# Attention values take a detour: rows scattered to DRAM by an index column, then read back

## The chip, the cores and the metric

The program runs on one core of one Trainium2 chip. The metric is device time in microseconds for one execution; lower is better. The five engines are written as in the profile: PE is the matrix engine, PEld its weight loads, DVE the vector engine, ACT the scalar engine, POOL the general-purpose engine, and SP the engine that issues most transfers. Each engine works through its own instruction list in order, and so does SP with its transfers: an instruction that waits holds up everything behind it on the same engine.

## The reference, cut to what matters

```python
# q, k, v: (4, 8, 768, 64) float32; proj: (64, 6)
q_bucket = sum((q @ proj > 0) * powers); k_bucket = the same for k
scores = where(q_bucket == k_bucket, q @ k.T / 8, -1e9)
attn = softmax(scores)
attn_out = attn @ v                       # v enters here, and only here
x = attn_out rearranged to (3072, 512)
out = relu(x @ w_in) ** 2 @ w_out         # 512 -> 2048 -> 512
```

There are 4 x 8 = 32 heads. For each head the values `v` are a matrix of 768 rows of 64 floats, that is of 256 bytes a row.

## The kernel before, in words

The kernel has two stages. The first is attention. It takes the 32 heads as 16 pairs (`pr` = 0 to 15), and each pair in 6 steps, one for each tile of 128 keys (`kt` = 0 to 5), so the stage is a loop over 96 steps `u` = 6 `pr` + `kt`. The second stage is the two products with `w_in` and `w_out`, written as a Strassen-like scheme of 128x256 products; nearly all of its time is PE (line 554).

The order of the work is written out by hand in the loop at lines 486 to 522. In step `u` stand, in this order: a running sum of exponentials on DVE (`add_up`, line 343); at `kt` = 0 the loads of queries and keys of pair `pr` + 2 (`load_pair`, eight transfers on SP, line 240); at `kt` = 2 the load of the values of pair `pr` + 1 (`load_values`, line 251); the scores of this step on PE (`score`, line 325) and their exponentials on ACT (line 330); preparation of the next pair's features; and the product with the values of the step two earlier (`attend`, line 353). So `attend(pr, 0)`, the first use of the values of pair `pr`, stands in step 6 `pr` + 2. When a pair is through, `normalize` (line 408) scales its output on DVE and stores it with one transfer on SP to `x_all` in DRAM (line 412).

Between these the stage also loads and rounds the weights of the second stage: 32 pieces, two for each pair. `load_weight` is one transfer on SP (line 122) into a ring of three buffers, so a load waits until DVE has rounded an earlier piece (`round_weight`, lines 159 to 166).

SP therefore sees, for each pair, always the same run of transfers: the values of the next pair, two weight pieces, four query and four key loads, the store of a finished pair's output, and then the values of the pair after. POOL does nothing after the first five microseconds: it makes the identity and other constants and loads `proj` twice (line 192).

`p_v`, the pool of the value tiles, has two buffers for each name.

Of the kernel before, what the change touches and what calls it, by code (L numbers as in the profile page):

```python
# [8 lines left out]
FP32 = mybir.dt.float32  # L9
BF16 = mybir.dt.bfloat16  # L10
I32 = mybir.dt.int32
U32 = mybir.dt.uint32
# [22 lines left out]
def kernel(  # L35
# [10 lines left out]
    nc = tc.nc  # L46
    PSUM = bass.MemoryType.PSUM

    B, H, S, D = q.shape
# [3 lines left out]
    P = 128  # L53
    SB = S // P
# [23 lines left out]
    p_d = ctx.enter_context(tc.tile_pool(name="p_d", bufs=1, space=bass.MemoryType.DRAM))  # L78
# [13 lines left out]
    p_v = first.enter_context(tc.tile_pool(name="p_v", bufs=2))  # L92
    const = first.enter_context(tc.tile_pool(name="const", bufs=1))
# [86 lines left out]
    lifts = const.tile([P, 1], FP32, name="lifts")  # L180
    excess = const.tile([P, 1], FP32, name="excess")
    ones = const.tile([P, 32], FP32, name="ones")
    picks = const.tile([P, P], FP32, name="picks")
    which = const.tile([P, 2, HS // 32], FP32, name="which")
    NRING = 4
# [2 lines left out]
    def constants():  # L188
        N = NBITS
        nc.gpsimd.memset(projs, 0.0)  # L190
        for h in range(2):
            nc.gpsimd.dma_start(out=projs[h * D:(h + 1) * D, 0:N], in_=proj)
        for t in (gains, lifts):
            nc.vector.memset(t, 0.0)
        nc.vector.memset(excess, -896.0)
        for h in range(2):
            r = h * D
            nc.vector.memset(gains[r:r + N + 1], -FAR / 2 * N)
            nc.vector.memset(gains[r:r + N], FAR / 2)
            nc.vector.memset(lifts[r:r + N + 1], 1.0)  # L200
            nc.vector.memset(lifts[r:r + N], -SMALL)
        nc.vector.memset(ones, 1.0)
        for e in ring:
            nc.vector.memset(e[:, :, S:S + 1], TINY)


        for g in range(4):
            cut = picks[:, g * 32:(g + 1) * 32]
            at = 64 * (g // 2)
            nc.gpsimd.tensor_tensor(  # L210
                out=cut, in0=ident[:, at:at + 32], in1=ident[:, at + 32:at + 64], op=ALU.add
            )
        nc.gpsimd.memset(which, 0.0)
        for g in range(4):
            nc.gpsimd.memset(which[g * 32:(g + 1) * 32, g % 2], 1.0)
# [6 lines left out]
    def load_first():  # L222

        for src, name in ((q, "q_nat"), (k, "k_nat")):
            t = p_qk.tile([P, SB, 2, D], FP32, name=name)
            for h in range(2):
                nc.sync.dma_start(
                    out=t[:, :, h], in_=src[0, h].rearrange("(p t) d -> p t d", t=SB)
                )
            nat[0, name] = t  # L230

    def load_pair(pr):


        b, j = divmod(pr, PB)
        for src, name in ((q, "q_nat"), (k, "k_nat")):
            t = p_qk.tile([P, S], FP32, name=name)
            for g in range(4):
                h, e = divmod(g, 2)
                nc.sync.dma_start(  # L240
                    out=t[g * 32:(g + 1) * 32].rearrange("i (t n d) -> i t n d", t=SB, n=P // 32),
                    in_=src[b, 2 * j + h].rearrange(
                        "(n i t) (e d) -> e i t n d", i=32, t=SB, e=2
                    )[e],
                )
            nat[pr, name] = t

    def load_values(pr):
        b, j = divmod(pr, PB)
        t = p_v.tile([P, 2, SB * D], FP32, name="v_nat")  # L250
        nc.sync.dma_start(
            out=t, in_=v[b, 2 * j:2 * j + 2].rearrange("h (p t) d -> p h (t d)", t=SB)
        )
        nat[pr, "v_nat"] = t

    def first_features(w, r):
# [214 lines left out]

    with tc.manual_schedule():
        load_first()
        load_values(0)
        make_identity(nc, ident)
        constants()
        for pr in range(1, AHEAD):
            load_pair(pr)
        for w in range(2):
# [6 lines left out]
        for u in range(len(steps) + 1):  # L486
            if 1 <= u <= len(steps):
                add_up(*steps[u - 1])
            if u < len(steps):
                pr, kt = steps[u]  # L490
                if kt == 0 and pr + AHEAD < NP:
                    load_pair(pr + AHEAD)
                if kt == 2 and pr + 1 < NP:
                    load_values(pr + 1)
                score(pr, kt)
# [398 lines left out]
```

## Time and profile before

| | us |
|---|---|
| median of 2 runs | 1002.38 (1002.13 to 1002.62) |
| the profiled execution, its own time | 1004.74 |
| the profiled execution, span from its first to its last instruction | 1002.6 |
| first stage, from the start to about | 407 |
| PE busy | 954.4 |
| DVE busy | 552.3 |
| ACT busy | 370.5 |
| POOL busy | 3.3 |

The span is what the profile's page divides into engines, slices and groups; the time of the execution is a little more than the span. The granted clock of PE was 0.992 of full speed over the whole run. In the lists of transfers, "us to landing" is the time from issue on the engine to the arrival of the last byte as its semaphore shows it.

### The profile page before, as it was taken

To read this page: it belongs to the slowest core of one execution; us is meant where nothing else is said; L and a number is where in the kernel's file an instruction comes from. 1 tells how busy PE (TensorE), PEld (TensorE's weight loads), DVE (VectorE), ACT (ScalarE), POOL (GpSimd) and SP (SyncE) were. 2 spreads that over 40 slices of the span, in tenths; PEclk is the share of its full clock that TensorE was granted. 3 is DMA by queue.
4 is the path that set the end of the run, shared out by engine and by line. 5 is a ranking of instruction groups with operands and counts; after the bars stand their busy time and mean duration, and the time that the engine had idled before them with its cause. 6 is when DMAs were issued, how large, how long until landed. Compare 5 with 4: busy or idle time off the path is not lost.

```text
span 1002.6 us, 12942 instructions
## 1 busy us (share of the span) xinstructions
PE 954.4 (95%) x5166; PEld 661.2 (66%) x5166; DVE 552.3 (55%) x1070; ACT 370.5 (37%) x689; POOL 3.3 (0%) x18
## 2 busy tenths in 40 slices
PE   6999999998889999899999999999999999999897
PEld 3333333333333333688888888888888888888786
DVE  1677777767777777795048406830682077116500
ACT  4666666665656665331023102300320132013200
POOL 1000000000000000000000000000000000000000
PEclk9999999999999999999999999999999999999999
DMA  8144545553553731001022102210311122000000
GB/s 188 29 115 112 113 107 127 130 125 97 116 139 84 157 122 37 17 1 42 22 76 72 43 22 85 63 53 22 90 49 63 29 71 90 22 22 1 1 22 23
DMA packets 121154, 70.11 MB, mean 70 GB/s; under 512 B 99328, under 2 KB 104448, under 8 KB 121088
## 3 DMA queue, kind: packets, MB, share of 16 engines
q1 hardware_dynamic: 121024, 69.22, 26.3%
q8 instruction: 42, 0.69, 0.3%
q14 instruction: 24, 0.20, 0.1%
q0 software_dynamic: 64, 0.00, 0.0%
HBM read 54.53 MB, written 14.68 MB: 69 GB/s over the span
## 4 chain that ended last, share of the span: by engine, by line
PE 63%; DVE 3%; ACT 1%; DMA 0%; issue 0%; SPq 0%; DVEq 0%; ACTq 0%
PE acc L554 58%; PE xo L353 2%; PE st L325 2%; DVE total L343 1%; PE tot L371 1%; DVE feat L273 0%; DVE x_t L408 0%; DMA q_nat<-in_q_dram 0%; DVE one L163 0%; DVE power L159 0%; PE near L285 0%; ACT small L147 0%; ACT power L148 0%; DVE flip L377 0%; DVE g L645 0%
## 5 line engine op out<-in xcount | busy, mean ns | idle before, releaser
L554 PE MATMUL acc<-x,w_in 128*128 128x256 f32 x768 | 174.7, 379 | 0.0
L330 ACT ACTIVATE e<-st 128x1024 f32<-128x1024 f32 x192 | 144.9, 806 | 75.8 <-PE st L325 75.8
L554 PE MATMUL acc<-w_out,g 128*128 128x256 f32 x768 | 170.4, 382 | 0.0
L554 PEld LDWEIGHTS acc<-w_out,g 128*128 128x128 f32 x768 | 147.0, 192 | 20.3
L554 PEld LDWEIGHTS acc<-x,w_in 128*128 128x128 f32 x768 | 145.8, 190 | 19.8
L325 PE MATMUL st<-feat,feat 64*128 64x512 f32 (+1 forms) x768 | 152.8, 489 | 0.0
L353 PE MATMUL xo<-e,v_nat 128*64 128x512 f32 (+1 forms) x768 | 145.8, 501 | 0.2 <-DVE x_t L408 0.2
L554 PE MATMUL acc<-t_x,s_in 128*128 128x256 f32 x576 | 133.9, 383 | 2.8 <-ACT one L561 2.8
L554 PE MATMUL acc<-t_out,gs 128*128 128x256 f32 x576 | 126.3, 379 | 0.0
L554 PEld LDWEIGHTS acc<-t_x,s_in 128*128 128x128 f32 x576 | 110.5, 192 | 18.6 <-ACT one L561 3.2
L554 PEld LDWEIGHTS acc<-t_out,gs 128*128 128x128 f32 x576 | 109.4, 190 | 14.9
L353 PEld LDWEIGHTS xo<-e,v_nat 128*64 128x64 f32 x768 | 47.2, 136 | 91.4 <-issue 89.0
L675 DVE TENSOR_TENSOR o<-acc,two 128x256 f32<-128x256 f32 x12 | 5.1, 425 | 155.9 <-PE acc L554 155.9
L325 PEld LDWEIGHTS st<-feat,feat 64*128 64x128 f32 x768 | 67.7, 191 | 34.7 <-issue 32.3
L343 DVE TENSOR_TENSOR total<-total,e 128x1536 f32<-128x1536 f32 x48 | 83.6, 1742 | 0.6 <-ACT e L330 0.4
L325 PE MATMUL st<-bits,bits 64*128 64x256 bf16 (+1 forms) x384 | 64.5, 330 | 19.6 <-ACT e L330 16.7
L645 DVE SCALAR_TENSOR_TENSOR g<-h 128x256 f32<-128x256 f32 x192 | 77.3, 423 | 4.9
L325 PEld LDWEIGHTS <-bits 64*128 64x128 bf16 x384 | 20.6, 94 | 84.8 <-issue 75.6
L561 ACT COPY two<-acc 128x256 f32<-128x256 f32 x60 | 22.4, 373 | 143.8 <-PE acc L554 143.8
L644 DVE TENSOR_TENSOR h<-acc,two 128x256 f32<-128x256 f32 x48 | 20.4, 425 | 54.2 <-PE acc L554 54.2
L377 DVE STREAM_TRANSPOSE flip<-tot 128x384 f32<-128x384 f32 x16 | 9.3, 583 | 69.7 <-PE tot L371 69.7
L561 ACT COPY one<-acc 128x256 f32<-128x256 f32 x60 | 22.3, 372 | 64.8 <-PE acc L554 64.8
(89 smaller groups left out, 716.9 us busy)
## 6 DMA issues: line engine op xcount, KB each, us to landing
raw<-in_moe_w_in_dram SPq DMA_DIRECT2D x16, 512.0 KB, 5.4
raw<-in_moe_w_out_dram SPq DMA_DIRECT2D x16, 512.0 KB, 4.5
v_nat<-in_v_dram SPq DMA_DIRECT2D x16, 384.0 KB, 5.6
x_all<-x_t SPq DMA_DIRECT2D x16, 384.0 KB, 3.4
x<-x_all SPq DMA_DIRECT2D x6, 1024.0 KB, 5.4
out_dram<-o SPq DMA_DIRECT2D x24, 256.0 KB, 2.0
raw_qk<-in_k_dram SPq DMA_DIRECT2D x16, 384.0 KB, 3.2
raw_qk<-in_q_dram SPq DMA_DIRECT2D x16, 384.0 KB, 3.1
```

What stands on the lines that cost most here:

```text
L325: nc.tensor.matmul(out=st[:, h, 0:hi - lo], lhsT=src[pr, 1][rows, key], rhs=src[pr, 0][rows, lo:hi], start=first, stop=not first,)
L330: nc.scalar.activation(out=e[:, :, lo:hi], in_=st[:, :, 0:hi - lo], func=ACTF.Exp, scale=scale)
L343: nc.vector.tensor_tensor(out=totals[pr], in0=in0, in1=weights[pr, kt][:, :, 0:S], op=ALU.add)
L353: nc.tensor.matmul(out=xo[h * D:(h + 1) * D, lo:hi], lhsT=nat[pr, "v_nat"][:, h, kt * D:(kt + 1) * D], rhs=weights[pr, kt][:, h, lo:hi], s ...
L371: nc.tensor.matmul(out=tot[g * 32:(g + 1) * 32, 0:HS], lhsT=ones, rhs=src[:, h, c * HS:(c + 1) * HS], start=src is totals[pr], stop=src is ...
L377: nc.vector.transpose(out=flip, in_=tot[:, 0:HS])
L554: nc.tensor.matmul(out=acc[to], lhsT=a(i), rhs=b(i), start=first and i == 0, stop=last and i == n - 1, skip_group_check=True,)
L561: nc.scalar.copy(out=t, in_=acc[of])
L644: nc.vector.tensor_tensor(out=h, in0=one, in1=two, op=ALU.add)
L645: nc.vector.scalar_tensor_tensor(out=out, in0=h, scalar=0.0, in1=h, op0=ALU.max, op1=ALU.mult)
L675: nc.vector.tensor_tensor(out=out, in0=one, in1=two, op=ALU.add)
```

## The change

The values of a pair are no longer loaded straight into the tile that PE reads. They are loaded into a tile `v_raw` of the same shape. Then, for each of the two heads, six transfers issued on POOL write them to a DRAM tile `v_rows`: each takes 128 rows of 256 bytes, one from each partition, and writes partition p's row at the row number that column `i` of `places` names. `places` is filled once by an `iota` on POOL with 128 i + p. One transfer on SP for each head then reads the 768 rows back into `v_nat`, in the arrangement that PE used before. Each head has a DRAM tile of its own. The call of `load_values(0)` moves behind `constants()`, so that `places` exists when it is used. Nothing is changed on PE, DVE and ACT.

```diff
+    places = const.tile([P, SB], U32, name="places")
...
+        nc.gpsimd.iota(places, pattern=[[P, SB]], base=0, channel_multiplier=1)
...
     def load_values(pr):
         b, j = divmod(pr, PB)
+        raw = p_v.tile([P, 2, SB * D], FP32, name="v_raw")
+        nc.sync.dma_start(
+            out=raw, in_=v[b, 2 * j:2 * j + 2].rearrange("h (p t) d -> p h (t d)", t=SB)
+        )
         t = p_v.tile([P, 2, SB * D], FP32, name="v_nat")
-        nc.sync.dma_start(
-            out=t, in_=v[b, 2 * j:2 * j + 2].rearrange("h (p t) d -> p h (t d)", t=SB)
-        )
+        for h in range(2):
+            rows = p_d.tile([S, D], FP32, name=f"v_rows{2 * pr + h}")
+            for i in range(SB):
+                nc.gpsimd.indirect_dma_start(
+                    out=rows, out_offset=bass.IndirectOffsetOnAxis(ap=places[:, i:i + 1], axis=0),
+                    in_=raw[:, h, i * D:(i + 1) * D], in_offset=None,
+                )
+            nc.sync.dma_start(
+                out=t[:, h].rearrange("p (t d) -> p t d", t=SB),
+                in_=rows.rearrange("(t p) d -> p t d", p=P),
+            )
         nat[pr, "v_nat"] = t
...
         load_first()
-        load_values(0)
         make_identity(nc, ident)
         constants()
+        load_values(0)
```

## The prediction

> **What bounds the kernel now.** I read the page's table of engines and its slices first: PE is busy 95% of the span, POOL 0%, and after slice 0 the POOL row is zeros.
>
> ```profile
> PE 954.4 (95%) x5166; PEld 661.2 (66%) x5166; DVE 552.3 (55%) x1070; ACT 370.5 (37%) x689; POOL 3.3 (0%) x18
> ...
> POOL 1000000000000000000000000000000000000000
> ```
>
> Then the chain of waits that ended last, in order of time. From 411.84 us on it is PE in the second stage, 531 us in one piece; that stage uses no values, so the change reaches it only through a later start. Before that the chain alternates between PE and DVE within each step, and a values transfer is not in it.
>
> ```profile
> 408.23 1.02 DVE x_t L408
> ...
> 411.84 531.19 PE acc L554 x2452
> ```
>
> Then the first stage, by the busy time of each engine over exactly one pair, and the timeline of the two `attend(pr, 0)` at its ends (pairs 1 and 2). A pair takes 23.67 us and PE works 22.52 of them, DVE 17.07, ACT 15.92, POOL nothing.
>
> ```profile
> 46.29:69.96 23.67, 22.52 (x156) 8.98 (x155) 17.07 (x24) 15.92 (x25) 0.00 (x0) 1.00 0.46 112
> ```
> ```profile
> 46.29 1.51 PE L353 MATMUL xo<-e,v_nat 128*64 128x512 f32 x8
> ...
> 69.96 1.51 PE L353 MATMUL xo<-e,v_nat 128*64 128x512 f32 x8
> ```
>
> By the same timeline `attend(15, 0)` is at 390.35, so the 14 pairs between took 344.1 us, 24.6 each. The change lengthens the way of the values, so I ask how early they start. The timeline of SP shows the run of transfers of one pair:
>
> ```profile
> 69.46 0.33 SPq L122 DMA_DIRECT2D raw<-in_moe_w_in_dram  x1
> 69.84 3.62 SPq L240 DMA_DIRECT2D q_nat<-in_q_dram  x4
> 73.50 2.77 SPq L240 DMA_DIRECT2D k_nat<-in_k_dram  x4
> 76.31 0.65 SPq L412 DMA_DIRECT2D x_all<-x_t  x1
> 77.05 0.38 SPq L251 DMA_DIRECT2D v_nat<-in_v_dram  x1
> ```
>
> The second weight load is let go by DVE at 69.46, and the values come 7.6 us behind it (8.0 in the pair before: 45.71 to 53.75; I take 7.7). The values of pair 2 are issued at 53.75 and used at 69.96: a lead of 16.2 us, for a transfer that lands in 5.6. Some 10 us of slack is all that the detour may cost. The list of transfers, and the tile view of `projs`, the only transfers that POOL issues now, give the prices:
>
> ```profile
> v_nat<-in_v_dram SPq DMA_DIRECT2D x16, 384.0 KB, 5.6
> out_dram<-o SPq DMA_DIRECT2D x24, 256.0 KB, 2.0
> q_nat<-in_q_dram SPq DMA_DIRECT2D x2, 192.0 KB, 3.2
> k_nat<-in_k_dram SPq DMA_DIRECT2D x2, 192.0 KB, 3.7
> projs<-in_proj_dram POOLq DMA_DIRECT2D x2, 1.5 KB, 3.1
> ```
> ```profile
> L192 POOL DMA_DIRECT2D projs<-in_proj_dram x2: 522/593/664, 1.7 to 2.4; - x2
> ...
> DMA to landing us min/median/max: 2.9/3.1/3.3
> ```
>
> The reader is to see that 1.5 KB issued on POOL took 3.1 us to land, as long as 192 KB issued on SP: such a transfer is nearly all fixed cost.
>
> **What the Trainium skill says.** "DMA: Bandwidth & Descriptors", "Anatomy of one DMA — SWDGE (gpsimd) path", gives a transfer issued on POOL about 2.0 us fixed plus its bytes at 436 GB/s, the fixed part mostly the confirmation that the last byte has landed, heaviest where it is written to HBM. The trace agrees on the kind of cost and has more, 2.9 to 3.3 us. The same page, "Two DMAs through the same engine are not ordered", says that order between transfers comes from waiting for the first one's completion; nothing in the trace of before shows such a wait on POOL. "SBUF — State Buffer", "SBUF: two separate sides", says that a DVE operation in a two-port mode, or with two SBUF inputs against a POOL operation that reads SBUF, shuts POOL out until it ends; POOL idles in this trace while DVE works, so no number here tests it.
>
> **The change part by part.** The instruction order of the changed program, with its waits, decides this. Per pair POOL has 12 scatters. The first waits for `v_raw`. Each later one waits for the one before to have landed, since all of a head write the same DRAM tile at places that are known only when it runs; only the seventh, the first of the second head, has no such wait. On SP each read-back waits for the last scatter of its head, and behind the second one stand two weight loads, eight query and key loads, the store, and only then the next `v_raw`. So the values of two pairs never overlap: after the second read-back of one pair is issued, SP goes through the run, loads, and POOL starts the next chain.
>
> Call s the time from one scatter to the next, and g the POOL time to issue one.
> - s is not in the trace. The nearest row is `projs`: 3.1 us to landing for 64 rows, 0.6 of it on POOL. A scatter has 128 rows; I double the 0.6, for s = 3.7. Below: the page's price of 2.0 plus 0.1 for 32 KB, or the lightest SP store, 2.0 (`out_dram`). Above: POOL must also fetch a row number for every row; I keep 6.0, about twice the landing of `projs`. The start-up traffic beside `projs` (transfer engines 0.90 busy in its first 20 us) makes 3.1 a little high, the fetched numbers make it low; I let these cancel. Being shut out by DVE adds up to 1.75 us to single scatters (line 343, the longest), but two-input DVE work is some 11 us of each pair's 24; part of the range.
> - Scatter chain of a pair: 6 s for the first head, the second starts one issue after the sixth begins, so 11 s + g = 40.7 + 0.6 = 41.3 us.
> - Period of a pair: read-back issue 0.7 (as for the q and k loads of line 227, two in 1.35), first weight load 0.5, second weight load to `v_raw` 7.7, landing 5.6, chain 41.3: 55.8 us. It needs no wait on PE or DVE: the query buffers, the output to store and the rounded weights it asks for belong to steps before the stalled `attend`. PE needs about 24 us of it and stands still for the rest. What is late next after that wait is the next one of its kind.
> - Start: `v_raw` 0 issued at 3.5 as now, landed at 9.1; `places` and the constants are ready by about 5, so the `iota` and the moved call cost nothing. Chain to 50.4. SP held until then: read-back 0.7, sixteen query and key loads 12.7 (4.23 to 16.95 now), two weight loads 1.2: `v_raw` 1 at 65.0, landed 70.6, chain to 111.9, and the read-back lands in 3.5 (the 192 KB rows above, 3.2 and 3.7): `attend(1, 0)` at 115.4 instead of 46.29.
> - Then 14 periods, of which the last has no query and key loads in it (6.5 less), plus 1.2 for the few other transfers in the run (lines 464, 516, 518): 14 x 55.8 - 5.3 = 775.9. `attend(15, 0)` at 891.3 instead of 390.35: 500.9 later.
> - All behind it, the last five steps and the second stage, is as before. PE may restart at a lower clock after each wait ("TensorE: Matmul & The Clock Gate", "Part 1: The HAM clock gate", halves it after idling; here the first matmuls of line 285 took 844 ns against 504 later): in the stage that falls into PE's idle time, and at its end it is under 3 us, which I leave out.
> - 6.3 MB more to DRAM and 6.3 MB back lie where the transfer engines are 0.46 busy now and would be half as busy: nothing.
>
> Sum: 1002.6 + 500.9 = 1503.5 us of span. The profiled execution's own time is 2.1 over its span, and the median of the runs 2.4 below that, so the median stands at the span: 1503. The sum holds 176 s (16 pairs of 11): each 0.1 us of s is 17.6 us.
>
> **The rivals.**
> - Scatters land fast. The store of 256 KB on SP in 2.0 us speaks for it, the 2.9 of the quickest POOL transfer against. With s = 2.0: 1503 - 176 x 1.7 = 1204.
> - The row numbers cost POOL dearly. That no row shows an indexed transfer speaks for it. With s = 6.0: 1908. POOL would then be busy for most of each pair rather than waiting.
> - Not slower: the waits between scatters turn out to hold nothing up, and 12 go out at 0.6 each, landing 3.1 after. The chain is 10.3 us and the period 0.7 + 0.5 + 7.7 + 5.6 + 10.3 = 24.8, against 24.6 now; with 7 us at the start, `attend(15, 0)` comes some 5 us late: 1008. It decides below s = 0.86 us, where the sum gives the old time. The instruction order speaks against it.
>
> **How the numbers follow.** 0.72 for the forecast (s from 2.6 to 5.3: 1309 to 1785), 0.11 for fast scatters, 0.14 for dear row numbers, 0.03 for the overlap. The range of 8 in 10 takes in some of both neighbours, s from 2.4 to 5.7: 1270 to 1850. What a measurement can tell from no change is 2%; only the overlap can end inside that or below, 0.02 within and 0.01 faster.
>
> **What would show it.** The profile after should have 192 scatters on POOL, about 3.7 us apart in elevens, PE waiting some 30 us before the first line 353 matmul of nearly every pair, PE's slices at about 4 over the first three fifths of the span, the period between `attend(pr, 0)` near 56, and a second stage that takes as long as now. A period under 35 us, PE waiting for something other than `v_nat`, or scatters that overlap would show me wrong.

## The result, and the profile after

The changed kernel takes 1363.92 us (median of 2 runs, 1363.64 to 1364.2), against 1002.38 before: 1.360 times as long, with a 95% interval of 1.357 to 1.363. The forecast was 1503, with 1270 to 1850 as its range and 0.97 on slower: the direction and the mechanism held, and the size came out 139 us too high.

The page of the changed kernel, its table of engines, two of its rows of slices, and the shares of the chain that ended last, by engine and by line:

```profile
PE 1011.8 (74%) x5166; PEld 673.1 (49%) x5166; DVE 554.1 (41%) x1070; ACT 369.2 (27%) x689; POOL 219.0 (16%) x211
...
POOL 4224223422332131342134000000000000000000
PEclk7857976887687597688768999999999999999999
...
PE 44%; DMA 26%; issue 25%; POOL 4%; DVE 1%; SPq 0%; ACT 0%; POOLq 0%; ACTq 0%; DVEq 0%
PE acc L568 43%; DMA v_rows<-v_raw,places 25%; POOL v_rows L260 4%; PE xo L367 1%; PE st L339 0%; DMA v_raw<-in_v_dram 0%; SPq L229 0%; DMA v_nat<-v_rows 0%; PE tot L385 0%; DVE g L659 0%; DVE x_t L422 0%; DVE recs L413 0%; DVE h L658 0%; ACT small L147 0%; ACT power L148 0%
```

POOL now works through the first 22 slices of 40, and the landing of scatters is a quarter of the chain although POOL is busy for 16% of the span: the scatters do not cost work, they cost waiting for each other. Another quarter, "issue", is time for which the view names no wait; its longest pieces, 10 to 35 us each, lie between two chains of scatters, where SP goes through its run and `v_raw` lands. PE's busy time rises from 954.4 to 1011.8 us with the same 5166 matmuls. In the stretch from 100 to 770 us its granted clock is 0.77 on average, against 0.99 in the first stage before, and a matmul of line 367 takes 553 ns in the mean where it took 501. This costs next to nothing here: PE waits again in every pair, and PE in the first stage is under 2% of the chain that ended last.

The second stage is untouched. In the chain in order of time it is 529.50 us in its long piece, against 531.19 before, and starts 361 us later; the span is 359.8 us longer:

```profile
772.84 529.50 PE acc L568 x2452
```

The list of transfers (size and median us to landing), the packets of POOL's queue, and what SP and DVE waited for (us in total, times, longest):

```profile
v_raw<-in_v_dram SPq DMA_DIRECT2D x16, 384.0 KB, 4.1
v_nat<-v_rows SPq DMA_DIRECT2D x32, 192.0 KB, 2.5
...
v_rows<-v_raw,places POOLq DMA_INDIRECT x192, 2.2
```
```profile
q0 software_dynamic: 6208, 6.31, 1.4%
```
```profile
SPq L264 <- DMA v_rows<-v_raw,places: 548.3, 32, 24.0
```
```profile
DVE w_in L439 <- DMA kept_in<-w_in: 38.0, 1, 38.0
```

SP waits 548.3 us for the scatters at its read-backs. A scatter lands in 2.2 us and lets the next one start 2.41 us after its own start; the forecast took 3.7 for both. The 192 scatters make 6144 of the 6208 packets, 32 each (the other 64 are the two loads of `proj`).

One period, from the second read-back of pair 4 to the first of pair 5, in the timeline (start, us, engine and line, tile, and in brackets the idle time before and what ended it):

```profile
226.49 0.37 SPq L264 DMA_DIRECT2D v_nat<-v_rows  x1
226.95 0.97 SPq L122 DMA_DIRECT2D raw<-in_moe_w_in_dram  x2
227.97 5.88 SPq L242 DMA_DIRECT2D q_nat<-in_q_dram  x4
229.03 2.83 PE L367 MATMUL xo<-e,v_nat 128*64 128x512 f32 x6 [12.15 <-DMA v_nat<-v_rows]
...
233.90 2.77 SPq L242 DMA_DIRECT2D k_nat<-in_k_dram  x4
...
236.71 1.70 SPq L426 DMA_DIRECT2D x_all<-x_t  x1
...
238.58 0.38 SPq L253 DMA_DIRECT2D v_raw<-in_v_dram  x1
...
242.29 0.97 POOL L260 DMA_INDIRECT v_rows<-v_raw,places  x1 [17.02 <-DMA v_raw<-in_v_dram]
...
244.70 0.97 POOL L260 DMA_INDIRECT v_rows<-v_raw,places  x1 [1.44 <-DMA v_rows<-v_raw,places]
247.11 0.97 POOL L260 DMA_INDIRECT v_rows<-v_raw,places  x1 [1.44 <-DMA v_rows<-v_raw,places]
...
254.34 2.30 POOL L260 DMA_INDIRECT v_rows<-v_raw,places  x1 [1.44 <-DMA v_rows<-v_raw,places]
256.95 1.16 POOL L260 DMA_INDIRECT v_rows<-v_raw,places  x1 [0.31 <-issue]
257.87 0.38 SPq L264 DMA_DIRECT2D v_nat<-v_rows  x1
```

This is the loop that the forecast described: read-back, SP's run of weights, queries, keys and store, `v_raw`, then the scatters, 2.41 us apart (0.97 of issue, 1.44 of waiting for the landing). Only the seventh, at 256.95, follows the sixth without a wait. PE begins `attend` with the first head at 214.94, just after that head's read-back landed, and waits another 12.15 us for the second head's. One line stands out: the scatter at 254.34 took 2.30 us of POOL instead of 0.97.

### The profile page after: what moved, and what is told of

Read it like the earlier page. It is cut to its first block, busy times and chain, and to the rows that moved or that the text cites. A ratio compares the mean times of both kernels' runs of the same rounds, so it can differ in the third digit from the quotient of the medians.

```text
span 1362.4 us, 13253 instructions
## 1 busy us (share of the span) xinstructions
PE 1011.8 (74%) x5166; PEld 673.1 (49%) x5166; DVE 554.1 (41%) x1070; ACT 369.2 (27%) x689; POOL 219.0 (16%) x211
## 3 DMA queue, kind: packets, MB, share of 16 engines
q0 software_dynamic: 6208, 6.31, 1.4%
## 4 chain that ended last, share of the span: by engine, by line
PE 44%; DMA 26%; issue 25%; POOL 4%; DVE 1%; SPq 0%; ACT 0%; POOLq 0%; ACTq 0%; DVEq 0%
PE acc L568 43%; DMA v_rows<-v_raw,places 25%; POOL v_rows L260 4%; PE xo L367 1%; PE st L339 0%; DMA v_raw<-in_v_dram 0%; SPq L229 0%; DMA v_nat<-v_rows 0%; PE tot L385 0%; DVE g L659 0%; DVE x_t L422 0%; DVE recs L413 0%; DVE h L658 0%; ACT small L147 0%; ACT power L148 0%
## 5 line engine op out<-in xcount | busy, mean ns | idle before, releaser
L367 PE MATMUL xo<-e,v_nat 128*64 128x512 f32 (+1 forms) x768 | 191.9, 553 | 275.4 <-DMA v_nat<-v_rows 250.2
L260 POOL DMA_INDIRECT v_rows<-v_raw,places x192 | 215.5, 1122 | 524.9 <-DMA v_raw<-in_v_dram 275.5
L367 PEld LDWEIGHTS xo<-e,v_nat 128*64 128x64 f32 x768 | 55.1, 147 | 399.5 <-DMA v_nat<-v_rows 213.5
L339 PE MATMUL st<-feat,feat 64*128 64x512 f32 (+1 forms) x768 | 164.7, 520 | 0.0
L339 PEld LDWEIGHTS st<-feat,feat 64*128 64x128 f32 x768 | 72.9, 205 | 39.4 <-issue 36.2
L339 PE MATMUL st<-bits,bits 64*128 64x256 bf16 (+1 forms) x384 | 68.8, 353 | 19.6 <-ACT e L344 16.0
L147 ACT ACTIVATE small<-power,excess 128x512 uint8<-128x512 uint32 x32 | 23.1, 722 | 94.5 <-DVE power L137 93.3
```

Of the source, the lines that this page charges most:

```text
L147: nc.scalar.activation(out=small, in_=power, func=ACTF.Relu, bias=excess)
L260: nc.gpsimd.indirect_dma_start(out=rows, out_offset=bass.IndirectOffsetOnAxis(ap=places[:, i:i + 1], axis=0), in_=raw[:, h, i * D:(i + 1) ...
L339: nc.tensor.matmul(out=st[:, h, 0:hi - lo], lhsT=src[pr, 1][rows, key], rhs=src[pr, 0][rows, lo:hi], start=first, stop=not first,)
L367: nc.tensor.matmul(out=xo[h * D:(h + 1) * D, lo:hi], lhsT=nat[pr, "v_nat"][:, h, kt * D:(kt + 1) * D], rhs=weights[pr, kt][:, h, lo:hi], s ...
```

## The experiments

All change one thing in the changed kernel unless it is said otherwise. Ratios are to the kernel before, on the same chip, with a 95% interval; the changed kernel's own is 1.360.

**1. Is it the wait between scatters?** `interleave` issues the scatters of the two heads in turn; both read-backs then come after all twelve.

```diff
-        for h in range(2):
...
-            for i in range(SB):
+        for i in range(SB):
+            for h in range(2):
                 nc.gpsimd.indirect_dma_start(
-                    out=rows, ...
+                    out=both[h], ...
```

> The scatters of the two heads of a pair are issued in turn (head 0, head 1, head 0, ...), nothing else changes; the read-backs come after all twelve. Theory (a pair waits for its chain of scatters, each of which waits 1.44 us for the landing of the one before it in its own head, after 0.97 us of issue): now the wait of one head lies under the issue of the other. Two scatters take about 2 x 1.27 = 2.54 us in place of 2 x 2.41, the twelve about 14 us in place of 28.3 from first to last start; the period of a pair falls from 47 to about 33 us and the time to about 1362 - 16 x 13.5 = 1146 us. Rival (a scatter costs what it costs, by its descriptors or its packets, and waiting is only what the profile shows of that): the chain stays at 28 us and the time at about 1360 us.

Measured: 1181.2 us, ratio 1.177 (1.167 to 1.187). The timeline of POOL in pair 4:

```profile
153.01 0.97 POOL L260 DMA_INDIRECT v_rows<-v_raw,places  x1 [18.48 <-DMA v_raw<-in_v_dram]
154.28 0.96 POOL L260 DMA_INDIRECT v_rows<-v_raw,places  x1 [0.31 <-issue]
155.55 0.97 POOL L260 DMA_INDIRECT v_rows<-v_raw,places  x1 [0.30 <-issue]
```

Most scatters are 1.27 us apart, all twelve the same work with the same packets, and 183 us are gone: the cost was the wait. The chain is 14.4 us from first to last start in this pair and 16.0 in the mean of 16 (28.1 before this edit), so the chains gave 193 us where I had 216; in the other pairs some scatters are stretched by DVE (experiment 5), by 22.5 us in all. The other 12 us by which the run came out later than its theory lie between the chains: from the last start of one to the first start of the next it is 301 us in all, against 286 in the changed kernel.

**2. Is it DRAM?** `plain_stores` writes each head with one transfer of fixed arrangement on SP instead of six scatters, both heads before the first read-back.

```diff
-            for i in range(SB):
-                nc.gpsimd.indirect_dma_start(
-                    out=rows, ...
+            nc.sync.dma_start(
+                out=both[h].rearrange("(t p) d -> p t d", p=P),
+                in_=raw[:, h].rearrange("p (t d) -> p t d", t=SB),
+            )
```

> The detour through DRAM stays, byte for byte, but each head is written by one transfer issued on SP with a fixed arrangement in place of six indexed ones on POOL. Theory (the POOL chain is the whole cost, DRAM is not): SP holds the pair for about 6 us of landing of v_raw, 3 us for the stores, and needs 10 us for its run: about 20 us, below the 24.6 us that PE needs. 1005 to 1025 us. Rival (writing to DRAM and reading back, with SP held behind the read-back, costs as such): over 1100 us.

Measured: 1009.7 us, ratio 1.006 (1.004 to 1.008). The same 6.3 MB go to DRAM and back. SP is held too, but for less long: 68.2 us in all at the stores, until `v_raw` has landed, and 29.7 at the read-backs, in place of 548.3. It costs 0.6%.

**3. Is it the bytes or the number?** `one_scatter_a_head` writes 128 rows of 1536 bytes with one scatter for each head.

```diff
-            rows = p_d.tile([S, D], FP32, ...)
-            for i in range(SB):
-                nc.gpsimd.indirect_dma_start(
-                    out=rows, out_offset=...(ap=places[:, i:i + 1], axis=0),
-                    in_=raw[:, h, i * D:(i + 1) * D], in_offset=None,
...
+            rows = p_d.tile([P, SB * D], FP32, ...)
+            nc.gpsimd.indirect_dma_start(
+                out=rows, out_offset=...(ap=places[:, 0:1], axis=0),
+                in_=raw[:, h], in_offset=None,
...
+            nc.sync.dma_start(out=t[:, h], in_=rows)
```

> One scatter for each head in place of six: 128 rows of 1536 bytes, at row number p, and the read-back takes the same rows; the same bytes pass through DRAM by the same index column. Theory (cost by the number of scatters that wait for each other): the two scatters of a pair are of different heads and do not wait, chain about 1.3 + 2.6 = 4 us, period 10 + 6 + 4 = 20 us, below PE's 24.6: 1003 to 1020 us. Rival (cost by bytes): six times the bytes in each of two scatters, the chain stays near 28 us, about 1360 us.

Measured: 1009.5 us, ratio 1.006 (1.004 to 1.008). The POOL time of a scatter (min, median and max ns, from the tile view of `v_rows`) and the landing (from the list of transfers):

```profile
L259 POOL DMA_INDIRECT v_rows<-v_raw,places x32: 970/974/2506, 8.0 to 379.1; - x32
```
```profile
v_rows<-v_raw,places POOLq DMA_INDIRECT x32, 2.6
```

Six times the bytes take the same 0.97 us on POOL and land in 2.6 us in place of 2.2. The cost goes by the number of scatters, hardly by their bytes; with two a pair that need not wait for each other, PE is busy for 95% of the span again. The read-back is simpler here too, with one row for each partition; `plain_stores`, which keeps the old read-back and takes as long, shows that the time did not go there.

**4. What stands between two chains, and what happens when it goes.** `raw_one_pair_ahead` loads `v_raw` and issues its scatters one pair earlier, before the read-backs of the pair before.

```diff
         load_values(0)
+        load_values(1)
+        read_back(0)
...
                 if kt == 2 and pr + 1 < NP:
-                    load_values(pr + 1)
+                    if pr + 2 < NP:
+                        load_values(pr + 2)
+                    read_back(pr + 1)
```

`load_values` here is `v_raw` and its twelve scatters, `read_back` the two transfers on SP.

> The load of v_raw and its twelve scatters are issued one pair earlier, ahead of the read-backs of the pair before, so SP no longer stands between two chains; the scatters still wait for each other. Theory (a period is the chain, 30.7 us to the last landing, plus 16.3 us of SP's run and the landing of v_raw that come between two chains): the 16.3 us go, the period becomes the chain alone, about 31 us, and the time about 1362 - 15 x 16 = 1122 us. Rival (PE's wait is set by POOL and transfer capacity shared with the other loads, so chains that lie beside the weight, query and key loads stretch by as much): over 1250 us.

Measured: 1201.0 us, ratio 1.197 (1.190 to 1.205). This was a miss of the theory by 79 us. The edit did what it should: POOL goes from one chain into the next with no gap. But a pair takes 36.8 us (514.9 us between the first scatters of pairs 1 and 15), not 31, since the scatters now lie beside SP's run:

```profile
109.75 0.37 SPq L270 DMA_DIRECT2D v_nat<-v_rows  x1
110.21 1.01 SPq L122 DMA_DIRECT2D raw<-in_moe_w_in_dram  x2
111.27 6.49 SPq L242 DMA_DIRECT2D q_nat<-in_q_dram  x4
111.36 0.97 POOL L261 DMA_INDIRECT v_rows<-v_raw,places  x1 [1.53 <-DMA v_rows<-v_raw,places]
117.81 2.84 SPq L242 DMA_DIRECT2D k_nat<-in_k_dram  x4
118.67 0.97 POOL L261 DMA_INDIRECT v_rows<-v_raw,places  x1 [6.34 <-DMA v_rows<-v_raw,places]
```

The scatter of 111.36 lets its successor go 7.31 us later, not 2.41. The rival, that chains beside the other loads stretch, was right in kind. Two further runs ask which loads. `ahead_no_qk` leaves out the query and key loads of pairs 3 to 15 (these pairs work on old tiles), and `ahead_no_weights` leaves out all weight loads but three.

```diff
 def load_pair(pr):                              # ahead_no_qk
+    if pr > 2:
+        for name in ("q_nat", "k_nat"):
+            nat[pr, name] = nat[pr - 2, name]
+        return
```
```diff
 def load_weight(i):                             # ahead_no_weights
+    if i >= 3:
+        raws[i] = held[i % 3]
+        return
...
+        held[i] = raw
```

> As raw_one_pair_ahead, but the query and key loads of pairs 3 to 15 are left out: these pairs work on the tiles of pairs 1 and 2, so 104 of SP's transfers of 96 KB, in rows of 128 bytes, are gone; all work on PE, DVE, ACT and POOL stays. In raw_one_pair_ahead the scatters of the first head lie beside SP's run of loads, and gaps of 2.4 us between them became 3 to 7.8; a pair took 36.8 us in place of the 31 forecast. Theory (the landing of a scatter is delayed by the packets of these loads): the gaps go back to about 2.6, the period to about 31 us, the time to about 1201 - 13 x 5.5 = 1130 us. Rival (the gaps come from DVE or from POOL itself, whose work now lies under DVE's all the time): the period stays at 36 to 37 us and the time within 15 us of 1201.

> As raw_one_pair_ahead, but of the 32 weight pieces of 512 KB only the first three are loaded and the others work on these three tiles; the query and key loads are there again, and all work on PE, DVE, ACT and POOL stays. With the query and key loads left out instead, the second scatter after SP's run still came 6.4 to 7.7 us after the first in most pairs, 115.97 against 109.43 in one, with two weight loads and v_raw issued at 107.15 to 108.82. Theory (the weight loads' 1 MB per pair is what a scatter lands behind): these gaps go back to about 3 us, the chain from 35 to about 31 us, the time to about 1201 - 14 x 4 = 1145 us. Rival (v_raw and the read-back itself, which are issued in the same microseconds, are enough): the gaps stay over 5 us and the time over 1180 us.

Measured: 1183.3 us, ratio 1.179 (1.169 to 1.189), without queries and keys; 1157.6 us, ratio 1.152 (1.146 to 1.158), without weights. The first expectation failed: some 18 us went (the two runs lie at 1175 and 1192) where 71 were forecast. The second came out 13 us above its theory of 1145. The gap between the second and the third scatter of a pair, which was 6.8 us in the mean of pairs 2 to 14 of `raw_one_pair_ahead`, stayed at 6.7 without the query and key loads and fell to 4.2 without the weights, and the period from 36.8 to 35.9 and 33.6 us. So the 1 MB of weights is the larger part of what a scatter lands behind, and the query and key loads a smaller one. The rest was not separated; the read-back and `v_raw` are issued in the same few microseconds. It is larger than the theory's 31 us suggests. That figure counted the last landing of a chain, but the next pair's first scatter writes another tile and follows after 1.3 us, so a chain as short as the changed kernel's 28.1 us would give a period of 29.4, against 33.6.

This fits with the 2.41 us between scatters in the changed kernel: there SP stands still at its read-back while most scatters run, so they have the transfer engines nearly to themselves. No run varies this alone.

**5. Does DVE shut POOL out?** `few_adds` leaves out three of the four additions of line 357 in each pair.

```diff
-        if kt == 0 or kt == SB - 1:
+        if kt != 1:
             return
```

> Three of the four additions of line 357 in each pair are left out (and 1.0 is added to the sums so that they stay away from zero). In the changed kernel POOL's issue of a scatter takes 0.97 us alone, and where one of these additions on DVE (1.75 us, two inputs from on-chip memory) is running it ends 0.84 us after the addition does; 25 of 192 scatters are so stretched, by 24.5 us together. Theory (DVE shuts POOL out): with three of four gone 15 to 20 us of stretch go, and as the chain is what PE waits for, as much of the time: about 1344 us. Rival (the stretch comes from traffic on the transfer engines and only coincides with the additions): the time stays at 1362 us, since PE and DVE have slack in every pair.

Measured: 1345.5 us, ratio 1.341 (1.338 to 1.343): 18 us less, as the theory had it. In the trace of the changed kernel, POOL and DVE side by side:

```profile
64.98 1.75 DVE L357 TENSOR_TENSOR total<-e,e 128x1536 f32<-128x1536 f32 x1
65.41 2.16 POOL L260 DMA_INDIRECT v_rows<-v_raw,places  x1 [1.43 <-DMA v_rows<-v_raw,places]
```
```profile
103.06 1.75 DVE L357 TENSOR_TENSOR total<-total,e 128x1536 f32<-128x1536 f32 x1
103.10 2.55 POOL L260 DMA_INDIRECT v_rows<-v_raw,places  x1 [16.46 <-DMA v_raw<-in_v_dram]
```

The additions end at 66.73 and 104.81, the scatters at 67.57 and 105.65: 0.84 us later both times. Issue time above 0.97 us is 29.6 us over the 192 scatters of the changed kernel and 15.3 in `few_adds`; of it, 24.5 and 9.5 stand under these additions alone. The Trainium skill, "SBUF — State Buffer", "SBUF: two separate sides", has such an exclusive lock, held for a whole instruction, for a DVE operation in a two-port mode, or one with two SBUF inputs against a POOL operation that reads SBUF. The trace agrees: of the 50 scatters that took over 1.0 us, 49 ended 0.84 or 0.85 us after the end of a DVE operation, 45 of them after one with two SBUF inputs (line 357, the weight rounding of lines 159 to 166, the sums of line 436). The other four ended so after the integer operations of lines 137 and 141, which have one SBUF input; whether these ran in a two-port mode the trace does not show. It agrees also on what does not lock: 19 scatters were issued beside nothing but a transposition (lines 287, 391, 413) or `x_t` (line 422), which read at most one input from SBUF, and none of them took over 1.0 us.

**6. The long period.** One gap between chains, from the second read-back to the next first scatter, was 34.2 us where the others were 9 to 20: DVE waited 38.0 us for `kept_in`, whose store stands on SP behind the second read-back of the tenth pair (pair 9, counted from 0), and SP's next weight load waited 19.4 us for DVE in turn. `late_sums` begins the sums over `w_in` six steps later; `before_late_sums` does the same to the kernel before.

```diff
-        w_steps.setdefault(W_IN + r * (SB - 1) + 1, []).append((sums_in, r))
+        w_steps.setdefault(W_IN + SB + r * (SB - 1) + 1, []).append((sums_in, r))
```

> The sums over w_in (line 439) begin six steps later than in the changed kernel, nothing else changes. In the changed kernel one period is 63.3 us in place of 47: DVE waits 38.0 us for the store kept_in, which stands on SP behind the second read-back of pair 10, and the next v_raw waits for what DVE does after it. Theory (this wait is in the time): the sums come when the store has long landed, the long period becomes a common one, and the time falls by about 16 us to 1346. Rival (the scatter chain hides it, another wait is next): the time stays within 5 us of 1362.

> The kernel before, with the sums over w_in six steps later. There DVE waits 5.5 us for the store kept_in in one step. Theory (slack of DVE hides most of it): 0 to 4 us faster, about 1000 us, close to what can be measured. Rival (the sums, moved towards the end of the stage, now fall on a busier DVE): up to 3 us slower.

Measured: `late_sums` 1344.7 us, ratio 1.340 (1.336 to 1.343), 19 us less; DVE no longer waits for `kept_in`, and the long gap is 19.4 us. `before_late_sums` 998.65 us, ratio 0.9955 (0.9939 to 0.9970): a little faster than the kernel before, and so the fastest version here.

**7. The repairs together.** `both_repairs` has the scatters in turn and one pair ahead, `both_repairs_late` also the later sums.

> Scatters of the two heads in turn, and v_raw with its scatters one pair ahead: both earlier edits together. Theory (period is the larger of PE's 24.6 us and the POOL chain, with nothing between two chains): the chain is about 17 us with DVE's interference, below 24.6, so PE is the bound again; 1005 to 1020 us, the rest being the later start of pair 0. Rival (SP, held at the read-backs, or DVE's interference stretches the chain beyond 24.6): 1050 us or more.

> both_repairs with the sums over w_in six steps later. In both_repairs the first use of the values of pair 15 comes 30 us later than in the kernel before, 9 of them at the start and about 15 where DVE waits for kept_in. Theory: the 15 go, about 1017 us. Rival (without that wait the scatter chain of 20 to 25 us is next and holds the same pairs): 1028 to 1033 us.

Measured: 1032.8 us, ratio 1.031 (1.026 to 1.035), then 1009.3, ratio 1.008 (1.005 to 1.011). The first came out above its theory and below its rival; the second shows that most of the missing part was the wait for `kept_in`. With all three, the 192 scatters and the detour cost 0.8% of the kernel before, and 1.3% by the two ratios if that kernel too has the later sums. The scatters of a pair take 15 to 25 us from first to last start in `both_repairs`, beside the loads and under DVE's locks; the mean, 20.9, lies within the 24.6 that PE needs.

**8. Where the price came from.** `pool_probe` is the kernel before with the load of `proj` on POOL repeated: six times beside SP's loads of the first stage, six times in the quiet second stage.

```diff
+    def probe(t):
+        nc.vector.memset(t, 0.0)
+        nc.gpsimd.dma_start(out=t[0:D], in_=proj)
...
+            if u % SB == 1 and 13 <= u < 49:
+                probe(spare_busy)
...
+                if i == 0 and r > 1:
+                    probe(spare_quiet)
```

> The kernel before with the load of proj, issued on POOL, repeated into a spare tile: six times in the first stage in the step in which SP issues its query and key loads, and six times in the first chunk of the second stage, where the transfer engines have little to do. Theory (the 3.1 us from which the forecast took the price of a scatter was mostly the traffic beside it): about 2.0 to 2.3 us to landing in the second stage, 3 us or more in the first. Rival (a direct load on POOL takes 3 us always, and the scatter, a store to DRAM, is the quicker form): about 3 us in both.

Measured, from the tile views of the two spare tiles (the same transfer, first beside the loads and then alone):

```profile
L184 POOL DMA_DIRECT2D spare_busy<-in_proj_dram x6: 516/517/532, 69.8 to 188.6; - x6
...
DMA to landing us min/median/max: 4.2/4.3/4.4
```
```profile
L184 POOL DMA_DIRECT2D spare_quiet<-in_proj_dram x6: 516/516/518, 431.4 to 461.6; - x6
...
DMA to landing us min/median/max: 1.7/1.9/2.5
```

The same 1.5 KB, issued in the same 0.52 us, land in 1.9 us alone and in 4.3 beside other loads; the transfer engines are busy for 0.10 of the one stretch (431 to 463 us) and 0.48 of the other (69 to 190). The 3.1 of the forecast lies between, taken at a start with much traffic.

## Why the prediction was right, and where its sum was off

The mechanism held: each scatter waits for the one before, SP holds its run behind the read-back, the values of two pairs do not overlap, PE stands still, and the second stage takes as long as ever. The experiments show the parts by changing one each: the wait (1), the indexed scatters against the bare detour (2), their number (3), the order on SP (4). That a head's scatters wait because their places are known only when they run, as the prediction says, no run tests.

The sum, up to the issue of the last read-back, by its terms:

| us | forecast | measured | difference |
|---|---|---|---|
| start to the first scatter | 9.1 | 8.3 | -0.8 |
| 16 chains, first scatter to second read-back | 660.8 | 484.2 | -176.6 |
| 15 gaps between chains | 217.9 | 253.7 | +35.8 |
| last read-back issued | 887.8 | 746.2 | -141.6 |

- **The step that was mis-sized is s.** I took 3.1 us from `proj` and added 0.6 for twice the rows. The time between scatters is 2.41 us in most cases and 2.64 in the mean of 160; with 176 of them, 1.06 us too many is 187 us. I had written that the start-up traffic "makes 3.1 a little high" and the fetching of row numbers makes it low, and let these cancel. They do not: the traffic was 1.2 of the 3.1 us (experiment 8), and the row numbers cost little: the issue is 0.97 us for 128 rows with an index against 0.52 to 0.66 for 64 rows without, less than twice.
- The skill's price, 2.0 us fixed ("DMA: Bandwidth & Descriptors", "Anatomy of one DMA — SWDGE (gpsimd) path"), which I held as the lower end, is what the trace shows for a transfer that is alone: 1.9 us for the load, 2.2 for the scatter.
- The POOL time g before the seventh scatter was 0.6 in the sum and is 1.70 in the mean, 1.27 where DVE is still: 18 us more over 16 pairs, contained in the 484.2. Part of it is the lock, which the prediction named for its range and did not put into the sum. The last landing of a chain, 2.17 us and not s, takes 8 us off again.
- The gaps: the wait for `kept_in` was missed. I had given the store 0.6 us of issue as one of "the few other transfers in the run" and did not ask who waits for it; moved behind a read-back, it held DVE for 38 us. Taking that away shortens the gaps by 15.9 us. The other 20 us are SP's run and the landing of `v_raw`, 15 to 16 us in most pairs where I had 14.5. The prediction's "needs no wait on PE or DVE" failed in the one pair with `kept_in`.
- Part of the closeness was luck. With s at its mean of 2.64 and all else as forecast, the sum gives 1503 - 187 = 1316; that g and the gaps were too low by 18 and 36 us hid part of the error in s. And 2.64 lies nearer to the 2.0 of the fast rival than to 3.7.
- Two signs came out otherwise. The period between `attend(pr, 0)` is 47.1 us, not 56. And PE does not wait some 30 us once in a pair: the first head has a read-back of its own, issued half a chain earlier, so in pair 4 PE waits 6.4 us before the first head and 12.2 before the second.
- The rivals: fast scatters at s = 2.0 gave 1204 and lay 160 us below; dear row numbers, 1908, were wrong, with POOL at 16%. The case that is hardly slower does exist, but another order of the scatters alone does not reach it (1181); it took all three edits of experiment 7 (1009), so the instruction order spoke against it rightly. By the sum it begins at s = 0.85, not 0.86.

## What to carry to other kernels

Transfers that each wait for the one before cost their landing times their number, hardly their bytes: look in the instruction order for waits between transfers into one tile whose places are not known at build time, and write fewer and wider ones, or alternate between two tiles. Take the price of a transfer from a row with the same traffic beside it. When a queue is held at a new wait, go through everything behind it and ask who waits for each, down to a single store.

## What the runs showed of the hardware that was not expected

- A transfer of 1.5 KB issued on POOL landed in 1.9 us alone and in 4.3 us beside the loads on SP's queue, though another engine issued these; a scatter beside SP's run of loads let the next one go after up to 7.8 us in place of 2.41, and after up to 7.7 with the query and key loads left out.
- An indexed scatter of 128 rows took POOL 0.97 us whether a row had 256 or 1536 bytes, and made 32 packets with rows of 256 bytes, as many as a load of 64 rows of 24 bytes, and 64 packets with rows of 1536.
- POOL's issue of a scatter that met a DVE operation with two SBUF inputs ended 0.84 or 0.85 us after that operation in 45 cases, and in four after an integer operation with one; beside nothing but transpositions it was not delayed.
